# The first batch and the second batch's attention of a fused attention and mixing kernel, traced by a list schedule

## The chip, the cores and the metric

The kernel runs on one core of one Trainium2 chip. The metric is the device time of one execution in microseconds (us). The engines are named as the profile names them: PE (matmuls), PEld (its weight loads), DVE, ACT, POOL (GpSimd) and SP, whose queue issues every DMA of this kernel.

## The reference

There are 8 batches of 576 tokens with 8 heads of 64, so 512 channels. Three stages follow each other:

```python
k_p, v_p = k, v averaged over 8 neighbouring tokens        # 72 keys per head
attn = softmax(q @ k_p.T / 8)
x = (attn @ v_p), heads side by side                        # 576 x 512 per batch
theta = x @ w_theta
y = w_tok_r @ (x * cos(theta)) + w_tok_i @ (x * sin(theta))
u = x + y
x = u + relu(u @ w_ch)
u = x + w_tok2.T @ relu(w_tok1.T @ x)                       # over the tokens
out = u + relu(u @ w_ch1) @ w_ch2
```

The weights of the mixing stages come as 64-bit floats. [...]

## The kernel before

Everything is traced by one Python function with the Tile framework, which derives the waits between engines and also chooses each engine's order: an instruction traced later can be placed ahead of one traced earlier, where Tile's own model finds the engine free. Every engine then works through its own list in order.

**Weights.** A weight is loaded in pieces of 128 rows by 256 or 288 columns: 8 of `w_theta` (`th`), 18 of `w_tok` (`tk`, 9 row blocks in two column halves). Each piece goes through one conversion, in `cq_ahead` and `cq_step`: ACT takes the absolute value of the high word (L223); a guard keeps it at 2^-15 or above, for these 26 pieces by a Relu with bias on ACT (L225) and an addition on POOL (L226); DVE shifts and masks (L256), puts the sign in (L262) and the low word's three bits (L268). A `tk` piece is then split into a high part (ACT, L294) and a low part `m - hi` (L296); two thirds of the low parts go to POOL, one third to DVE (`lo_engine`). The later weights (`w_ch` and on) take their guard on DVE, by a maximum (L253).

**One batch.** `emit_sc` multiplies queries by a block diagonal of summed keys (`bdk`), takes the row maximum (DVE, L539), subtracts it (DVE, L540) and exponentiates (ACT, L545), four times for two heads each; `emit_norm` sums (DVE, L552) and scales (POOL, L557); `emit_pt` transposes on PE, `emit_av` multiplies by the values into `R`. `emit_theta` gives theta for 5 groups (half 0: groups 2, 0, 1; half 1: groups 0, 1); `emit_z` transposes `R` and multiplies it by cosine and sine (DVE, L758), and splits the product into high (ACT, L772) and low parts (L773, POOL or DVE). The mix is 8 accumulations of 27 matmuls (`mix_part`) over `Z` and the split `w_tok`, added to `R` on DVE (L811) and stored. Batch 0 uses plain 32-bit matmuls for attention and theta; from batch 1 on high and low parts are multiplied apart.

**Order.** `prologue` traces batch 0 up to `Z` of half 0, with the conversion of pieces spread between by counts (`P["pq"]`). PE fills some waits with matmuls on a constant tile (`keep_busy`, L169). Then comes a loop over the batches: the 72 steps of `mix_steps(b)` are the main line, and everything else (theta and `Z` of half 1 of batch b; attention, theta and `Z` of half 0 of batch b+1; loads and sums of keys and values of batch b+2) is a side list with due times from `P`, put between the steps by `interleave`. For batch 0 the due times are those of `f_`. After the last batch the channel mixing of w_ch, the second token mix and the two large channel products follow.

**Buffers.** There is one home for each tag. Raw pieces stay in `Z0`, `kr`, `stg0`, `stg1`, `R1`, `w0` to `w3` and `Z1` until they are converted; batch 1's keys come into `Xl` when batch 0's values are pooled, its values into `R1`. There are 8 PSUM banks: 4 `x`, 2 `t`, 2 `m`.

Of the kernel before, what the change touches and what calls it, by code (L numbers as in the profile page):

```python
# [9 lines left out]
F32 = mybir.dt.float32  # L10
# [34 lines left out]
    "pl": (2.0, 2.0, 0, 0.0),  # L45
    "l_cq": (1.26, 1.0),
    "l_u": (11.67, 22.91, 4.84),
    "l_th1": (3.39, 3.6),
# [4 lines left out]
    "a_th": (0,),  # L53
    "a_tr": 4,
    "md": (1.7, 2.0),
    "pq": (2.0, 2.0, 2.0, 2.0, 3.6, 2.0, 2.0, 2.0, 2.0, 2.0, 20.0),
    "mo": 1,
}
F64_FLOOR = 2.0 ** -15
TH = ((0, 256), (256, 320))  # L60
HL3 = ((0, 0), (0, 1), (1, 0))


@with_exitstack
def tile_attn_moe(
# [11 lines left out]
    w_ch1: bass.AP,  # L77
    w_ch2: bass.AP,
    consts: bass.AP,
    k1: bass.AP,  # L80
    v01: bass.AP,
    pool: bass.AP,
    out: bass.AP,
# [111 lines left out]
    def cq_use(stages, cvts):  # L195
        cq_bufs[:] = list(stages)
        cvt_bufs[:] = list(cvts)
# [1229 lines left out]
            second_chunk(c)  # L1427


    def prologue():  # L1430
        z0 = st("Z0", [128, 7, CV, 2], U32, "early0")
        z1 = st("Z1", [128, 6, CV, 2], U32, "early")
        r1 = st("R1", [128, 4, CV, 2], U32, "early2")
        kr = st("kr", [128, 2, CV, 2], U32, "early4")
        zt = st("zt1", [128, 3, CV], F32, "early3")
        cv = st("vr", [128, 3, CV], F32, "early5")
        ws = [st(W_TAGS[i], [128, CV, 2], U32, f"early_w{i}") for i in range(4)]
        cq_use([(z0[:, i],) for i in range(7)] + [(kr[:, i],) for i in range(2)] + ["stg0", "stg1"]
               + [(r1[:, i],) for i in range(4)] + [(w,) for w in ws] + [z1[:, i] for i in range(6)],
               ["cvt0"] + [zt[:, i] for i in range(3)] + [cv[:, i] for i in range(3)])  # L1440
        pq = [int(x + 0.5) for x in P["pq"]]
        pl = [int(x + 0.5) for x in P["pl"]]
        add_wth()
        add_wtk()
        kt = {}
        for p in range(4):
            if p % 2 == 0:
                kt[p // 2] = st(f"pt{p // 2}", [128, 2, T], F32, f"k{p // 2}")
                q_t[0, p // 2] = st(f"q{p // 2}", [128, 2, TD], F32)
            nc.sync.dma_start(out=kt[p // 2][:, p % 2], in_=kT[0, p])  # L1450
            nc.sync.dma_start(out=q_t[0, p // 2][:, p % 2], in_=qT[0, p])
            cq_load(pl[p])
        load_pool()
        load_n(0, vn_t, "Xl", v01[0])
        cq_load()
        for p in range(4):
            ks = st("sums", [128, 72], F32)
            nc.vector.tensor_reduce(
                out=ks, in_=kt[p // 2][:, p % 2].rearrange("p (k o) -> p k o", o=8), axis=AX.X, op=ALU.add
            )  # L1460
            for e in range(2):
                pr = slice(64 * e, 64 * e + 64)
                nc.vector.tensor_copy(out=bdk[pr, p, 72 * e:72 * e + 72], in_=ks[pr])  # L1463
            emit_sc(0, p)
            if p > 0:
                emit_norm(0, p - 1)
        pool_v(0)
        emit_norm(0, 3)
        pool_vl(0)
        cq_step(pq[0])  # L1470
        emit_pt(0, 4)
        emit_pt(0, 0)
        for j in range(4):
            if j < 3:
                emit_pt(0, j + 1)
            flush()
            for th in range(2):
                emit_av(0, j, th)
            cq_step(pq[1 + j])
        flush()  # L1480
        cq_step(pq[5])
        emit_theta(0, 0, 2)
        emit_theta(0, 0, 0)
        cq_step(pq[6])
        flush()
        emit_z(0, 0, 2, nc.gpsimd)
        emit_theta(0, 0, 1)
        cq_step(pq[7])
        flush()
        emit_z(0, 0, 0, nc.gpsimd)  # L1490
        cq_step(pq[8])
        flush()
        emit_z(0, 0, 1, nc.vector)
        flush()
        cq_step(pq[9])
        if B > 1:
            open_vlo()
            for g in range(2):
                load_q(1, g)
            load_n(1, kn_t, "Xl", k1)  # L1500
            load_n(1, vn_t, "R1", v01[1])
        cq_step(pq[10])

    def side_first():
        ft = P["f_prep"]
        return [
            (ft[0], lambda: pool_k(1, 0)),
            (ft[1], lambda: pool_k(1, 1)),
            (ft[2], lambda: pool_v(1)),
            (ft[3], lambda: pool_vl(1)),  # L1510
        ] + [(P["f_ws"][0] + i * P["f_ws"][1], lambda i=i: split_wth(i)) for i in range(4)]

    def side_next(b):
        n = b + 1
# [24 lines left out]
        ]  # L1539

    if True:
        prologue()
        for b in range(B):
            last = b == B - 1
            side = []
            f = "l_" if last else "f_" if b == 0 else ""
            for g, a, z, lo in zip((0, 1), P[f + "th1"], P[f + "z1"], (nc.gpsimd,) * 2):
                side.append((a, lambda g=g: emit_theta(b, 1, g)))
                side.append((z, lambda g=g, lo=lo: emit_z(b, 1, g, lo)))
            if not last:  # L1550
                side += side_next(b)
            if b + 2 < B:
                side += side_load(b + 2)
            if b == 0 and not last:
                side += side_first()
# [68 lines left out]
def _layout(inputs):  # L1624
# [25 lines left out]
    for r in range(128):  # L1650
# [9 lines left out]
        "consts": consts, "k1": nat[0][1], "v01": nat[1], "pool": pool,  # L1660
    }


# [20 lines left out]
```

## Time and profile before

| | |
|---|---|
| median of 3 runs | 1298.02 us (1297.08 to 1298.23) |
| the profiled execution's own time | 1297.42 us |
| its span, first to last instruction | 1295.6 us |
| busy: PE, DVE, ACT, POOL | 1254.6, 956.9, 661.0, 321.9 us |
| the chain that ended last | PE 76%, DVE 9%, DMA 2% |

A busy engine is one with an instruction running. The timeline merges neighbouring instructions of one kind into one row (xN), with its start, its length, and the idle time ahead of it in brackets with what ended it. Each 32-bit matmul leaves two records. Rows of neighbouring instructions overlap a little, since an instruction's end is later than the next one's start.

### The profile page before, as it was taken

The page shows a single profiled execution, that of the slowest core. Times are in us where ns is not written, and L with a number is a line of the kernel's source. Part 1 is how long each engine was busy: PE and PEld are TensorE (multiplying, and loading weights), DVE is VectorE, ACT ScalarE, POOL GpSimd, SP SyncE. Part 2 cuts the span into 40 slices and gives each one's busy share as a digit, 9 for nine tenths or more (in the row PEclk, how much of TensorE's full clock was granted, in tenths as well). Part 3 has the DMA queues.
Part 4 walks back from the last instruction along what each step waited for, and adds up shares of the span by engine and source line. Part 5 has one row for each costly group of instructions (what it writes and reads, how often), then busy time and mean ns, then how long its engine had stood idle before and what let it go on. Part 6 is the DMA issues. An engine that isn't in the chain of part 4 may idle for free.

```text
span 1295.6 us, 22271 instructions
## 1 busy us (share of the span) xinstructions
PE 1254.6 (97%) x8130; PEld 1209.8 (93%) x8132; DVE 956.9 (74%) x1730; ACT 661.0 (51%) x1256; POOL 321.9 (25%) x339
## 2 busy tenths in 40 slices
PE   5799999999999999999999999999999999999998
PEld 4489999999999988899999998999999999999998
DVE  7888577585857796686775689996545598987893
ACT  4776565666666573333331356655544444444442
POOL 4643425232332532111110012320000032123122
PEclk9899999999999999999999999999999999999999
DMA  9424233231321023556683388885438966547621
GB/s 338 158 71 138 74 100 103 75 94 62 115 73 52 36 93 109 181 199 233 246 297 116 128 273 281 281 280 178 146 123 279 367 215 224 172 142 218 196 91 62
DMA packets 120382, 214.50 MB, mean 166 GB/s; under 512 B 11536, under 2 KB 66320, under 8 KB 120272
## 3 DMA queue, kind: packets, MB, share of 16 engines
q1 hardware_dynamic: 120272, 213.08, 49.2%
q8 instruction: 64, 1.05, 0.3%
q14 instruction: 46, 0.38, 0.1%
HBM read 134.39 MB, written 78.64 MB: 164 GB/s over the span
## 4 chain that ended last, share of the span: by engine, by line
PE 76%; DVE 9%; DMA 2%; issue 2%; ACT 2%; POOL 0%; SPq 0%; ACTq 0%; DVEq 0%; POOLq 0%
PE m L159 28%; PE x L159 25%; PE t L159 19%; PE x L173 3%; DMA ws<-w_ch 1%; DMA scr_x<-u 1%; DVE wm L1024 1%; DVE raw_n L1155 1%; DVE wm L1028 1%; DVE wsum L1039 0%; DVE p L1313 0%; DVE g L1323 0%; ACT wo L1052 0%; DVE ope_R L1152 0%; ACT wm L1018 0%
## 5 line engine op out<-in xcount | busy, mean ns | idle before, releaser
L159 PE MATMUL m<-wtk,Z 128*128 128x256 f32 (+1 forms) x1536 | 253.6, 301 | 4.6 <-ACT Z L772 3.0
L159 PEld LDWEIGHTS m<-wtk,Z 128*128 128x128 f32 x1536 | 220.2, 190 | 6.1 <-ACT Z L772 3.2
L773 POOL TENSOR_TENSOR Z<-tmp,Z 128x1024 fp32r<-128x1024 f32 x31 | 74.9, 2415 | 112.1 <-ACT Z L772 112.1
L159 PE MATMUL x<-ope_Z,wa 128*128 128x384 f32 x492 | 95.4, 337 | 0.0
L1404 POOL TENSOR_TENSOR o<-o,u 128x384 f32<-128x384 f32 x12 | 16.3, 1379 | 285.5 <-DVE u L1392 218.0
L159 PEld LDWEIGHTS x<-ope_Z,wa 128*128 128x128 f32 x492 | 86.8, 188 | 0.1
L1038 POOL TENSOR_TENSOR wsum<-wm 128x128 f32<-128x128 f32 (+1 forms) x18 | 15.1, 840 | 272.4 <-DVE wm L1028 264.8
L758 DVE TENSOR_TENSOR tmp<-x,tmp 128x1024 f32<-128x1024 f32 x32 | 39.1, 1221 | 33.4 <-ACT tmp L734 17.8
L159 PE MATMUL t<-wth,Xh 128*128 128x256 f32 x448 | 62.9, 282 | 0.0
L159 PE MATMUL x<-bdk,q 128*128 128x144 f32 x320 | 47.8, 303 | 11.5 <-DVE bdk L1463 7.0
L159 PEld LDWEIGHTS t<-wth,Xh 128*128 128x128 f32 x448 | 57.9, 188 | 0.9 <-DVE tmp L709 0.2
L159 PEld LDWEIGHTS x<-bdk,q 128*128 128x128 f32 x320 | 44.5, 203 | 13.1 <-issue 10.9
L159 PE MATMUL m<-wtk,zt 128*128 128x256 f32 (+1 forms) x192 | 56.8, 296 | 0.0
L557 POOL TENSOR_TENSOR e<-e,sm 128x720 f32<-128x720 f32 x32 | 44.7, 1398 | 20.8 <-DVE sm L556 18.7
L159 PE MATMUL t<-ope_Z,wa 128*128 128x384 f32 x234 | 48.2, 336 | 1.5 <-ACT p L1312 1.5
L159 PE MATMUL m<-ope_Z,wa 128*128 128x384 f32 x234 | 48.2, 336 | 0.0
L740 DVE SCALAR_TENSOR_TENSOR tmp<-tmp,t 128x512 f32<-128x512 f32 x33 | 22.5, 683 | 31.3 <-ACT tmp L727 31.3
L545 ACT ACTIVATE e<-e 128x720 f32<-128x720 f32 x32 | 25.6, 804 | 38.0 <-DVE e L540 37.9
L159 PE MATMUL x<-ope_R,wa 128*128 128x384 f32 x228 | 44.1, 338 | 0.4 <-DVE p L1317 0.3
L811 DVE TENSOR_TENSOR R<-m,R 128x256 f32<-128x256 f32 (+1 forms) x64 | 28.8, 450 | 20.2 <-PE m L159 20.2
L772 ACT CAST Z<-tmp 128x1024 fp32r<-128x1024 f32 x32 | 33.4, 1043 | 20.0 <-DVE tmp L758 20.0
L159 PE MATMUL m<-ope_Xl,wa 128*128 128x384 f32 x204 | 42.9, 338 | 0.6 <-ACT ope_Xl L1151 0.6
(406 smaller groups left out, 3546.3 us busy)
## 6 DMA issues: line engine op xcount, KB each, us to landing
wa<-scr_w SPq DMA_DIRECT2D x42, 512.0 KB, 5.6
scr_g<-g SPq DMA_DIRECT2D x108, 192.0 KB, 3.0
scr_w<-wo SPq DMA_DIRECT2D x42, 256.0 KB, 3.0
scr_u<-R SPq DMA_DIRECT2D x32, 288.0 KB, 2.1
u<-scr_u SPq DMA_DIRECT2D x32, 288.0 KB, 4.0
scr_w<-wo SPq DMA_DIRECT2D x18, 512.0 KB, 3.4
scr_x<-u SPq DMA_DIRECT2D x32, 288.0 KB, 2.4
raw_n<-scr_x SPq DMA_DIRECT2D x24, 384.0 KB, 4.3
```

The lines of the kernel that those rows point to most:

```text
L159: nc.tensor.matmul(out=o, lhsT=l, rhs=r, start=start, stop=stop, skip_group_check=skip)
L173: nc.tensor.transpose(o, i, ident)
L545: nc.scalar.activation(out=ep, in_=ep, func=ACTF.Exp, scale=1.0 / 64.0)
L557: nc.gpsimd.tensor_tensor(out=ep, in0=ep, in1=sm.unsqueeze(3).to_broadcast([128, 5, 2, 72]), op=ALU.mult)
L740: nc.vector.scalar_tensor_tensor(out=t, in0=t, scalar=MAGIC, in1=pt, op0=ALU.subtract, op1=ALU.subtract)
L758: nc.vector.tensor_tensor(out=tmp, in0=px.unsqueeze(1).to_broadcast([128, 2, 512]), in1=tmp, op=ALU.mult)
L772: nc.scalar.copy(out=zh, in_=zv)
L773: later(1.0 if lo is nc.vector else 0.0, lambda: lo.tensor_sub(out=zl, in0=zv, in1=zh.bitcast(F32)), tg, zg)
L811: nc.vector.tensor_add(out=R[:, j, ts], in0=o, in1=R[:, j, ts])
L1024: nc.vector.scalar_tensor_tensor(out=xu, in0=t[:, :, :, 1], scalar=0xC0000000, in1=xu, op0=ALU.bitwise_and, op1=ALU.bitwise_or,)
L1038: nc.gpsimd.tensor_tensor(out=s[:, 2], in0=a11, in1=a21, op=ALU.subtract)
L1404: nc.gpsimd.tensor_tensor(out=u22[d].t, in0=u22[d].t, in1=u2[d].t, op=ALU.add)
```

## The change

`prologue` and batch 0's turn of the batch loop, with its side list, are replaced by `first_batches`. It describes the whole work of batch 0 (attention, the 26 pieces, theta and `Z` of both halves, the mix, its stores), the split of `w_theta`, and of batch 1 loads, attention, theta and `Z` of half 0, with the loads of batch 2's queries and its key sums, as operations with dependencies, a duration in ns, an engine (sometimes a choice of two), the buffers and the banks they take. `Plan.run` goes through time in that model: of all operations that could start within 20 ns of the earliest, it traces the one with the longest chain behind it. POOL operations and DVE operations marked `True` aren't started together (`lock`). Afterwards each instruction of PE, DVE, ACT and POOL gets a dependency without a semaphore on the one traced before it on its engine; SP's don't. Values of batch 2 are loaded and summed behind the last of them (`issue_after`), and the batch loop starts at batch 1.

What the operations are differs from before in this: all 26 guards are one DVE maximum (`GUARD`), so L225 and L226 have none left; all 18 low parts of `tk` are on POOL (`LOWS` is empty); of batch 0's half 0 all three low parts of `Z` are on DVE (`ZL`), the scaling of head pairs 2 and 3 of batch 0 is on DVE (`EDVE`); small copies out of PSUM are on DVE or ACT as the plan finds it. `keep_busy` fills the waits of PE that the plan foresees up to the first mix matmul, and the time ahead of the first matmul. Keys of batch 1 are loaded in four column blocks. The host passes both batches' natural keys (`k01`).

```diff
+GUARD = range(26)
+LOWS = ()
+WS = (0, 1)
+ZL = (1, 1, 1)
+EDVE = (2, 3)
+NEAR = 20.0
...
-    def prologue():
...
+        LAT = {"PE": 170.0, "DVE": 110.0, "ACT": 120.0, "POOL": 110.0, "SP": 0.0}
...
+                    for w in o["ways"]:
+                        if w[0] == "SP":
+                            if sp:
+                                continue
+                            sp = True
+                        s = max(ready, free[w[0]], lock + (90.0 if w[0] == "POOL" else 0.0) if w[2] is True else 0.0)
+                        d = w[1]
+                        if w[2] in ("exp", "sin") and w[2] != table:
+                            d += 1290.0
+                        best.append((s, s + d, o, w))
+                s0 = min(b[0] for b in best)
+                near = [b for b in best if b[0] <= s0 + NEAR]
+                top = max(b[2]["rank"] for b in near)
...
+                if e == "PE":
+                    idle(s, s - free["PE"])
...
+                if e == "SP" and w[2]:
+                    self.dma = max(self.dma, s + 3000.0) + w[2] * 1000.0 / 370.0
+                    o["end"] = self.dma
...
+    def first_batches():
...
+        def idle(s, ns):
+            if started[0] is False:
+                started[0] = True
+                keep_busy(dump, int((s - WARM) / 440.0))
+            elif started[0]:
+                keep_busy(dump, int(max(0.0, ns - 60.0) / 217.0))
...
+            o = add(("ACT", ac(n), False, absf), [at], hs, take=mids)
+            if i in GUARD:
+                o = add(("DVE", n * 0.521 + 65, True, most), [o], hs)
...
+            o = add(("DVE", n * 0.521 + 65, True, shl), [o], hs)
+            o = add(("DVE", dv(n), True, sign), [o], hs)
+            o = add(("DVE", dv(n), True, low3), [o], hs)
...
+            x = add(("ACT", ac(n), False, hi), [o], hs + [w], give=[hold])
+            ways = [("POOL", po(n), True, low(nc.gpsimd))]
+            if i in LOWS:
+                ways = [("DVE", dv(n), True, low(nc.vector))]
...
+        for p in range(4):
+            scores(0, p)
+        for i in range(8):
+            add_piece(i)
+        values(0)
+        transposed(0, 4)
         for j in range(4):
...
+        for i in range(8, 26):
+            add_piece(i)
+        for g in TG:
+            theta(0, 0, g)
+        for g in range(2):
+            theta(0, 1, g)
+
+        fetch_q(1)
+        kn[1] = home("Xl", [128, 5, 512], F32, "nat_k1")
+        kt_at[1] = fetch_tail(kn[1], k01[1])
+        for p in range(4):
+            fetch_k_pair(1, p)
+            fetch_q_pair(1, p)
+        fetch_v(1, "R1")
...
+        pl.run(idle)
...
+        for i in nc.cur_bb.bb.instructions[first:]:
+            k = str(i.engine)
+            if "SP" in k:
+                continue
+            if k in seen:
+                tc.add_manual_dep(i, seen[k], mybir.DependencyInfo(
+                    mybir.DependencyClass.NoSync, mybir.DependencyReason.DATA), reason="the plan's order")
...
     if True:
-        prologue()
-        for b in range(B):
+        behind = first_batches()
+        with ExitStack() as s:
+            for i in behind:
+                s.enter_context(tc.issue_after(i))
+            if B > 2:
+                load_v(2, 0)
+                load_vl(2)
+                prep_v(2, 0)
+                load_v(2, 1)
+                prep_v(2, 1)
+                prep_vl(2)
+            flush()
+        for b in range(1, B):
```

## Rows read from the trace of the kernel before

**Rows 1.** The page's 40 slices of 32.4 us: busy tenths of PE.

```profile
PE   5799999999999999999999999999999999999998
```

**Rows 2.** Busy time of each engine by stretch; a stretch, its length, engines with counts.

```profile
core 0: us, PE busy (x) PEld busy (x) DVE busy (x) ACT busy (x) POOL busy (x), PEclk, DMA share, GB/s
0.00:78.20 78.20, 57.21 (x244) 40.56 (x247) 65.87 (x150) 50.08 (x111) 44.13 (x64) 0.95 0.63 214
78.20:142.01 63.81, 62.30 (x435) 57.40 (x434) 47.93 (x89) 39.00 (x78) 24.35 (x24) 0.99 0.34 108
142.01:205.00 62.99, 62.95 (x491) 62.01 (x490) 40.41 (x79) 38.38 (x75) 19.84 (x20) 1.00 0.27 87
445.00:505.00 60.00, 54.51 (x401) 52.77 (x400) 53.99 (x130) 34.43 (x74) 23.64 (x28) 0.97 0.31 102
```

**Rows 3.** Timeline of PE, 0 to 80 us: start, length, instruction, idle ahead.

```profile
5.50 2.74 PE L159 MATMUL x<-bdk,q 128*128 128x144 f32 x10 [5.50 <-DVE bdk L1463]
...
22.72 1.39 PE L159 MATMUL x<-bdk,q 128*128 128x144 f32 x10
...
40.32 0.59 PE L169 MATMUL x<-busy 128*128 128x512 bf16 x2
40.75 0.38 PE L173 MATMUL x<-con,e 128*128 128x128 f32 x2
...
55.88 7.61 PE L159 MATMUL t<-wt,R 128*128 128x512 f32 x18 [5.77 <-DVE R L523]
...
64.44 3.72 PE L159 MATMUL t<-wt,R 128*128 128x256 f32 x16 [0.51 <-DVE tmp L740]
...
78.21 0.99 PE L159 MATMUL m<-wtk,Z 128*128 128x256 f32 x2
```

**Rows 4.** Timeline of PE from 139 us on: the first matmul behind batch 0's mix.

```profile
142.01 1.11 PE L159 MATMUL t<-wth,Xh 128*128 128x256 f32 x8
```

**Rows 5.** Groups of PE, 0 to 142.01 us: busy us, mean ns, idle before.

```profile
L169 PE MATMUL x<-busy 128*128 128x512 bf16 x38 | 11.0, 379 | 1.2 <-ACT pt L588 1.2
...
L159 PE MATMUL x<-nat_Xl,pool 128*128 128x512 f32 (+1 forms) x10 | 5.8, 712 | 0.2 <-PE x L159 0.2
```

**Rows 6.** Groups of DVE, 0 to 142.01 us.

```profile
L256 DVE TENSOR_SCALAR early<-early 128x288 uint32<-128x288 uint32 (+1 forms) x22 | 9.0, 422 | 0.0
...
L552 DVE TENSOR_REDUCE ss<-e 128x10 f32<-128x720 f32 x8 | 7.1, 897 | 1.0 <-ACT e L545 1.0
...
L296 DVE TENSOR_TENSOR wtk<-early,wtk 128x288 fp32r<-128x288 f32 x6 | 4.9, 818 | 3.8 <-ACT wtk L294 3.8
...
L430 DVE TENSOR_REDUCE vls<-vlr 96x64 f32<-96x512 f32 x6 | 4.0, 675 | 0.5 <-POOL vlsh L434 0.5
L398 DVE TENSOR_REDUCE sums<-kr 128x144 f32<-128x1152 f32 x3 | 4.0, 1346 | 0.0
...
L408 DVE TENSOR_REDUCE sums<-vr 128x128 f32<-128x1024 f32 x2 | 2.4, 1214 | 0.0
...
L773 DVE TENSOR_TENSOR Z<-tmp,Z 128x1024 fp32r<-128x1024 f32 x1 | 1.2, 1210 | 0.0
```

**Rows 7.** Groups of ACT, 0 to 142.01 us.

```profile
L225 ACT ACTIVATE early<-early,floor 128x288 f32<-128x288 f32 (+1 forms) x22 | 11.2, 523 | 0.2
```

**Rows 8.** Groups of POOL, 0 to 142.01 us.

```profile
L226 POOL TENSOR_SCALAR early<-early 128x288 f32<-128x288 f32 (+1 forms) x22 | 13.6, 622 | 17.6 <-ACT early L225 17.3
...
L296 POOL TENSOR_TENSOR wtk<-early,wtk 128x288 fp32r<-128x288 f32 x10 | 8.8, 896 | 0.8 <-ACT wtk L294 0.8
...
L226 POOL TENSOR_SCALAR cvt<-cvt 128x256 f32<-128x256 f32 (+1 forms) x4 | 3.2, 799 | 5.5 <-ACT cvt L225 5.5
```

**Rows 9.** Timeline of DVE: one guard of a later weight.

```profile
77.53 2.33 DVE L253 TENSOR_SCALAR cvt<-cvt 128x256 f32<-128x256 f32 x1
```

**Rows 10.** Timeline of POOL at the same time.

```profile
77.31 2.41 POOL L773 TENSOR_TENSOR Z<-tmp,Z 128x1024 fp32r<-128x1024 f32 x1
```

**Rows 11.** Timeline of SP's queue: the load of batch 1's values.

```profile
51.66 0.89 SPq L457 DMA_DIRECT2D nat_R<-v  x2
```

More of the change, by code (lines that the diff above doesn't have):

```diff
@@ L60 @@
 TH = ((0, 256), (256, 320))
+TG = (2, 0, 1)
+GUARD = range(26)
+NK = 4
+WARM = 800.0
+LOWS = ()
[3 more added lines that the diff above has]
+NEAR = 20.0
 HL3 = ((0, 0), (0, 1), (1, 0))
@@ L1504, in side_first, with __init__, add, home @@
[L1504 to L1511, printed above, removed]
+    class Plan:
+        LAT = {"PE": 170.0, "DVE": 110.0, "ACT": 120.0, "POOL": 110.0, "SP": 0.0}
+        def __init__(self):
+            self.ops = []
+            self.users = {}
+            self.dma = 3400.0
+        def add(self, ways, deps=(), homes=(), take=None, give=()):
+            if isinstance(ways, tuple):
+                ways = [ways]
+            o = dict(ways=ways, deps=list(deps), take=take, give=give)
+            for h in homes:
+                o["deps"] += h.prior
+                h.users.append(o)
+            self.ops.append(o)
+            return o
+        def home(self, tag, shape, dt, name=None):
+            return Home(self, tag, shape, dt, name)
+        def run(self, idle):
+            table = None
+            for o in self.ops:
+                o["rank"] = 0.0
+            for o in reversed(self.ops):
+                e, ns = o["ways"][0][0:2]
+                o["rank"] += (ns if e != "SP" else 2000.0) + self.LAT[e]
+                for d in o["deps"]:
+                    d["rank"] = max(d["rank"], o["rank"])
+            free = {e: 0.0 for e in self.LAT}
+            lock = 0.0
+            todo = list(self.ops)
+            while todo:
+                best = []
+                sp = False
+                for o in todo:
+                    if any("end" not in d for d in o["deps"]):
+                        continue
+                    ready = max([0.0] + [d["end"] for d in o["deps"]])
+                    if o["take"] is not None:
+                        if not o["take"].free:
+                            continue
+                        ready = max(ready, o["take"].free[0][0])
+                    for w in o["ways"]:
+                        if w[0] == "SP":
+                            if sp:
+                                continue
+                            sp = True
[7 more added lines that the diff above has]
+                top = max(b[2]["rank"] for b in near)
+                o = [b[2] for b in near if b[2]["rank"] == top][0]
+                s, end, o, w = min((b for b in best if b[2] is o), key=lambda b: b[1])
+                todo.remove(o)
+                e = w[0]
+                if e == "PE":
+                    idle(s, s - free["PE"])
+                free[e] = end
+                if w[2] is True:
+                    lock = end
+                elif w[2] is not False and e == "ACT":
+                    table = w[2]
+                o["end"] = end + self.LAT[e]
+                if e == "SP" and w[2]:
+                    self.dma = max(self.dma, s + 3000.0) + w[2] * 1000.0 / 370.0
+                    o["end"] = self.dma
+                if o["take"] is not None:
+                    o["take"].last = o["take"].free.pop(0)[1]
+                w[3]()
+                for g in o["give"]:
+                    g.done(o["end"])
@@ new lines, in tile_attn_moe, with __init__, __call__ @@
+    class Home:
+        def __init__(self, plan, tag, shape, dt, name):
+            self.prior = plan.users.get(tag, [])
+            self.users = plan.users[tag] = []
+            self.args = (tag, shape, dt, name)
+            self.t = None
+        def __call__(self):
+            if self.t is None:
+                self.t = st(*self.args)
+            return self.t
+    class Slots:
+        def __init__(self, names):
+            self.free = [(0.0, n) for n in names]
+            self.last = None
@@ L1553, in tile_attn_moe @@
                 side += side_load(b + 2)
-            if b == 0 and not last:
-                side += side_first()
             if last:
@@ L1659, in _layout @@
         "w_ch1": w["moe2_w_ch1"], "w_ch2": w["moe2_w_ch2"],
-        "consts": consts, "k1": nat[0][1], "v01": nat[1], "pool": pool,
+        "consts": consts, "k01": nat[0], "v01": nat[1], "pool": pool,
     }
```

688 lines of the change are left out of this document (618 added, 70 removed).

## The prediction

> **What bounds the kernel now.** I began with the slices: PE is at nine tenths almost everywhere, and the large hole is in the first two [rows 1]. The windows then place it. From 142.01 us on PE is busy 62.95 of 62.99 us [rows 2], so the kernel is a PE line with a ragged start, and what the start loses moves the end one for one. The boundary at 142.01 is the first matmul of batch 1's turn, behind the last of batch 0's mix [rows 4]; 78.20 is where that mix begins [rows 3]. A later hole, 445 to 505 us, where PE is busy 54.51 of 60 and DVE 53.99 [rows 2], belongs to the last batch; the change does not touch it and it only shifts.
>
> Next I asked how much of the first 142.0 us is work of PE that has to be done. Busy are 57.21 + 62.30 = 119.5 us [rows 2], so 22.5 are idle. Of the busy time some is no work:
> - The filler matmuls: 38 of them [rows 5], and two take 40.75 - 40.32 = 0.43 us [rows 3], so 38 x 0.215 = 8.2 us.
> - The slow clock: the scores of the first head pair take 2.74 us, those of the last 1.39 [rows 3]. Three pairs ran slow, 3 x 1.35 = 4.0 us. The theta block at 55.88 us comes behind 5.77 us of idling and takes 7.61; at the pace of the one at 64.44 (16 records of 256 columns in 3.72 us, 0.23 each) its 8 records of 512 and 10 of 256 would be 26 x 0.23 = 6.0. That is 1.6 more.
>
> So 119.5 - 8.2 - 5.6 = 105.7 us are work and **36.3 us are not**. The reason is in the groups and the timeline of DVE's neighbours: PE waits for DVE (at 5.50 for `bdk`, at 55.88 for `R`, at 64.44 for `tmp` [rows 3]), and DVE is busy 65.87 of the first 78.20 us, against 50.08 of ACT and 44.13 of POOL [rows 2]. In the second stretch DVE is at 47.93 of 63.81 while PE is full. The two engines take turns as the bound: about 114 us of DVE work and 106 us of PE work in 142. Better overlap of these two is what the plan could give.
>
> **The change part by part.** All edits act on that start, so I price DVE and PE up to the new place of 142.01, which I call T.
>
> *DVE, removed.* Six low parts go to POOL, 6 x 0.818 = 4.9 us [rows 6]. Work for later batches that was placed inside the first 142 us isn't in the plan, or follows it by `issue_after`: six value sums of 0.675 (4.0), one of the three key sums of 1.346 (1.3, the plan keeps batch 2's two), two value sums of 1.214 (2.4) [rows 6], and the w_ch guard of 2.33 [rows 9]. Together 10.0. This comes later, where DVE has slack (40.41 busy of 62.99 us [rows 2]) under a full PE; if that cover were gone it would cost at most its own 10.0 back.
>
> *DVE, added.* 26 guards. No guard of these pieces ran on DVE before. From below: nothing, where DVE would have waited. From above: 2.33 us each, the one later guard I see [rows 9], 60.6 in all. The nearest row is the shift of the same pieces, also one input and one output of the same size, at 0.422 us [rows 6]; I take it: 26 x 0.422 = 11.0. Two low parts of Z more on DVE: 1.210 for the one with 1024 columns [rows 6] and half of it for the one with 512, 1.8. Two scalings of 720 columns, at the 0.897 of the sum over the same 720 [rows 6]: 1.8. The choice of engine for small copies I cost at nothing, since it goes either way and ACT has room.
>
> DVE's sum: 113.8 - 4.9 - 10.0 + 11.0 + 1.8 + 1.8 = 113.5 us. So the title's edits hardly change DVE's load; what changes is its idling, 28.2 us of the 142 before.
>
> *ACT and POOL.* ACT loses the Relus, 11.2 us for 22 of 26 [rows 7]. POOL loses 26 additions, 13.6 + 3.2 = 16.8, and gains 6 x 0.896 = 5.4 [rows 8], and hands the two Z parts and two scalings to DVE. Neither is the bound (89 and 68 of 142 us [rows 2]), so both are worth nothing by themselves. They take two engine crossings from each piece's chain, so DVE finds its next piece ready.
>
> *PE.* The work stays 105.7 us. The warm-up before the first matmul and the fillers in foreseen waits cost nothing while DVE is the bound, and spare the 5.6 us of slow clock; the cover is PE's own idling, and where the plan foresees a wait that isn't there, one filler costs 0.215.
>
> *SP.* The same bytes, with two DMAs more for keys and values and a tiny one for the pool matrix ahead of the first keys. I cost the tiny one at its own issue, at most half of the 0.89 for a pair [rows 11], 0.4 us, on the path to the first scores. Batch 1's loads need homes that are freed by conversions, as before.
>
> **Two floors for T.** DVE: it starts near 4.5 us (PE's first matmul at 5.50 waits for it) and needs 113.5, so T is 118 at the least. PE: in the first 30 us it has only scores (4 x 1.39 = 5.6 [rows 3]) and the pooling of values (5.8 [rows 5]), 11 us, since everything else waits for the softmax; the other 94.7 follow, so T is 125 if it is never idle behind 30 us, and some 121 if the plan brings the softmax forward by 4 us, which DVE's sum allows because no conversion need stand in its way. Before, the loss behind 30 us was 142.0 - 30 - 94.7 = 17.3 us. I assume that the plan leaves 5 of it above the floor of 121, as 26 pieces, PSUM banks and two `tmp` tiles still couple the engines. **T = 126, a gain of 16 us**: 1297.42 of the profiled execution becomes 1281.4; the median of the runs is 0.6 above that execution, so 1282.0.
>
> **A rule weighed.** A guard of 256 columns that began at 77.53 us took 2.33 us and ended at 79.86; beside it POOL ran a subtraction from 77.31 to 79.72 [rows 9, 10]. So a DVE instruction can stand until POOL's ends. The Trainium skill, "SBUF — State Buffer", section "SBUF: two separate sides", says that DVE and GpSimd share one port pair under an exclusive lock held for a whole instruction, and that DVE takes it in its 2-port modes or with two SBUF inputs against a GpSimd instruction that reads SBUF. By that rule all four DVE steps of a piece, not only the guard, stop for each low part. It speaks against putting all low parts on POOL; the trace agrees in this one pair of rows. By the rule T is rival 1's below. My sum leaves collisions at the rate already in the 0.422 and gives 126.
>
> **The rivals.**
> 1. *Each low part on POOL stops DVE for its whole length.* 18 x 0.896 = 16.1 us [rows 8] on top of 113.5, so DVE's floor is 134 and T about 135: a gain of 7, 1291. For it: rows 9 and 10. Against it: the 26 additions, which collided too, leave POOL, and the plan keeps the marked operations apart, so that POOL can work while DVE reads PSUM. Chance 0.12. The Trainium skill's rule above gives this time wherever the plan's durations don't hold on the chip.
> 2. *The change doesn't do what it says for the order.* The added dependencies order only the plan's own instructions. Tile can still put later batches' sums between them, as it did (six of 0.675, for instance). Then DVE gets its 10.0 back and order is no better coordinated: T 136 to 142, a gain of 0 to 6, 1292 to 1298. Chance 0.12, a third of it within the noise.
> 3. *Slower: PE stands behind a transfer of batch 1.* PE works its list in order. The plan puts batch 1's keys and values wherever its model of the DMAs (370 GB/s, 3 us) lets them be, possibly ahead of theta or of the mix. The values were issued at 51.66 us [rows 11], because `R1` had to be emptied of four pieces; if PE reached them at 30 and they come near 55, it stands 25 us with all of theta queued behind it. T would be 151, 9 us slower: 1307. It decides once such waits exceed the 16 us of my gain. For it: SP's queue is in order too, and one late conversion delays all loads behind. Against it: the plan's chain lengths put theta and conversions first, and all pieces but a few arrive well before they are needed. Chance 0.11.
> 4. *Better: PE full from 25 us on*, T 118 or less, DVE at its floor: 1273 or less. Chance 0.07.
>
> **How the numbers follow.** The forecast, 1274 to 1290, has 0.58. Faster by over 0.2% (2.6 us, about what a measurement here can tell from no change): 0.58 + 0.07 + 0.12 + two thirds of 0.12, so 0.85. Within 0.2%: 0.05. Slower: 0.10 (a hundredth of rival 3 lies within the noise). The range reaches to 1271 below (T = 115, under both floors by little) and to 1298 above, which takes in rivals 1 and 2 and leaves out rival 3 and the far end of rival 4.
>
> **What would show it.** Right: the first mix matmul some 10 us earlier or more, batch 1's scores and key pooling ahead of it, the first matmul of batch 1's turn near 126, no PE idling of 5 us behind 30, first scores at 1.4 rather than 2.7 us, L225 and L226's successors on DVE near 0.4 us, and behind T the pace of before. Wrong: guards and shifts near 1 us (rival 1), later batches' sums among the plan's (rival 2), a PE wait on a DMA (rival 3). The forecast fails if DVE still idles over 20 us before T, or if PE's line behind T is longer than before.

## The result, and the profile after

The changed kernel takes **1275.4 us** (median of 4 runs, 1274.72 to 1276.8) against 1298.01 of the kernel before in the same job: ratio 0.983, 95% interval 0.981 to 0.985. The forecast was 1282.0, between 1271 and 1298. The profiled execution took 1276.8 us; its span, from the first to the last instruction, is 1275.0.

The page's slices of PE (40 of 31.9 us), which answer to [rows 1]; the dip at the fifteenth slice is the later hole of batch 7, now 20 us earlier:

```profile
PE   8999999999999989999999999999999999999998
```

Busy time by stretch in the changed kernel: a stretch, its length, then PE, PEld, DVE, ACT and POOL with their counts, the granted TensorE clock, the DMA share and GB/s. 52.39 us is the first mix matmul (before 78.21), 121.78 the first matmul of batch 1's turn, which the prediction called T (before 142.01 [rows 4]).

```profile
0.00:52.39 52.39, 47.20 (x216) 31.20 (x216) 43.67 (x115) 33.20 (x83) 13.79 (x20) 1.00 0.90 295
52.39:121.78 69.39, 67.43 (x463) 62.50 (x464) 55.63 (x119) 48.33 (x108) 33.64 (x25) 0.98 0.24 77
...
0.00:121.78 121.78, 114.63 (x678) 93.69 (x679) 99.31 (x233) 81.52 (x190) 47.42 (x44) 0.99 0.52 171
...
22.97:121.78 98.81, 95.07 (x594) 83.39 (x594) 83.57 (x193) 71.98 (x167) 43.02 (x35) 0.98 0.43 137
...
121.78:185.00 63.22, 61.15 (x460) 59.59 (x459) 48.28 (x92) 38.84 (x79) 22.18 (x25) 0.97 0.42 131
425.00:485.00 60.00, 54.43 (x392) 52.66 (x391) 53.89 (x133) 31.39 (x70) 26.06 (x28) 0.94 0.29 91
```

**Where the gain is.** T came 142.01 - 121.78 = 20.2 us earlier, and the span is 1295.6 - 1275.0 = 20.6 us shorter; behind T the line is as long as before (1295.6 - 142.0 = 1153.6, now 1153.2). Up to T, PE idled 142.0 - 119.5 = 22.5 us before [rows 2] and 121.8 - 114.6 = 7.2 now, which is 15.3 us; the other 4.9 are busy time (119.5 to 114.6) with as many records (679 before, where those at 78.20 count twice, and 678 now), of which 38 and 40 are fillers. So the same matmuls were done faster: the slow scores are gone, and the clock fell less. All the idling that went stood ahead of the first mix matmul: 78.2 - 57.2 = 21.0 us before, 52.4 - 47.2 = 5.2 now.

The timeline of PE in the changed kernel shows both, and what stands behind T:

```profile
5.72 1.48 PE L167 MATMUL x<-bdk,q 128*128 128x144 f32 x10 [0.59 <-ACT bdk L1768]
...
22.97 1.23 PE L181 MATMUL x<-con,e 128*128 128x128 f32 x9
...
36.03 7.07 PE L167 MATMUL x<-wt,R 128*128 128x256 f32 x32
...
52.39 0.62 PE L167 MATMUL m<-wtk,Z 128*128 128x256 f32 x3 [1.08 <-ACT Z L2193]
...
57.53 1.50 PE L167 MATMUL t<-pool,nat_k 128*128 128x16 f32 x12
...
61.31 0.90 PE L167 MATMUL x<-bdk,q 128*128 128x144 f32 x6
...
121.78 1.10 PE L167 MATMUL t<-wth,Xh 128*128 128x256 f32 x8
...
133.62 1.42 PE L167 MATMUL x<-bdk,q 128*128 128x144 f32 x6 [2.06 <-DVE tmp L766]
```

The first scores take 1.48 us where they took 2.74 [rows 3]; the transposes of the softmax begin at 22.97, and batch 1's key pooling (57.53) and scores (61.31) now stand behind the first mix matmul; theta runs 32 matmuls in one row (7.07 us, 0.22 each) with no wait ahead of it, where 5.77 us of idling stood before. The longest wait between 36 us and T is the 1.08 at the first mix. Behind T a new wait of 2.06 us has come, for DVE's `tmp`. In the kernel before, the transposes began 5.8 us later than now:

```profile
28.76 0.38 PE L173 MATMUL x<-con,e 128*128 128x128 f32 x2
```

The groups of DVE from 0 to 121.78 us (line, operation, tiles, shapes, count, then busy us, mean ns, idle before), which answer to [rows 6]: the guard (L1697), the shift (L1708), and two of the five steps of a w_ch piece (L276, L261).

```profile
L1697 DVE TENSOR_SCALAR early<-early 128x288 f32<-128x288 f32 x16 | 5.1, 339 | 1.1 <-ACT early L1694 1.1
L1708 DVE TENSOR_SCALAR early<-early 128x288 uint32<-128x288 uint32 x16 | 4.7, 327 | 0.0
...
L1697 DVE TENSOR_SCALAR early<-early 128x256 f32<-128x256 f32 x6 | 1.5, 283 | 0.0
...
L276 DVE SCALAR_TENSOR_TENSOR cvt<-stg,cvt 128x256 uint32<-128x256 uint32 x1 | 1.4, 1389 | 0.0
...
L261 DVE TENSOR_SCALAR cvt<-cvt 128x256 f32<-128x256 f32 x1 | 1.2, 1212 | 0.0
```

The group of POOL that answers to the second of [rows 8], the low part:

```profile
L1741 POOL TENSOR_TENSOR wtk<-early,wtk 128x288 fp32r<-128x288 f32 x16 | 18.5, 1173 | 33.1 <-ACT wtk L1738 31.4 <-DVE tmp L2180 1.7
```

### The profile page after: what moved, and what is told of

The parts are those of the page before. It is cut to its first block, busy times and chain, and to the rows that moved or that the text cites. A ratio compares the mean times of both kernels' runs of the same rounds, so it can differ in the third digit from the quotient of the medians.

```text
span 1275.0 us, 22259 instructions
## 1 busy us (share of the span) xinstructions
PE 1248.5 (98%) x8132; PEld 1205.9 (95%) x8132; DVE 953.2 (75%) x1739; ACT 656.4 (51%) x1264; POOL 302.7 (24%) x301
## 4 chain that ended last, share of the span: by engine, by line
PE 76%; DVE 11%; DMA 7%; ACT 2%; issue 2%; SPq 1%; POOL 0%; DVEq 0%; ACTq 0%; POOLq 0%
PE m L167 28%; PE x L167 26%; PE t L167 19%; PE x L181 3%; DMA ws<-w_ch 1%; DMA early<-w_tok 1%; DMA scr_x<-u 1%; DMA early<-w_theta 1%; DMA scr_w<-wo 1%; DMA k<-kT 1%; DMA q<-qT 0%; DMA vr<-vm 0%; DMA scr_g<-g 0%; DVE early L1713 0%; DMA stg<-w_ch 0%
## 5 line engine op out<-in xcount | busy, mean ns | idle before, releaser
L167 PE MATMUL m<-wtk,Z 128*128 128x256 f32 (+1 forms) x1536 | 259.6, 304 | 5.7 <-ACT Z L780 3.0
L167 PE MATMUL x<-ope_Z,wa 128*128 128x384 f32 x492 | 94.8, 336 | 0.0
L781 POOL TENSOR_TENSOR Z<-tmp,Z 128x1024 fp32r<-128x1024 f32 x26 | 62.9, 2419 | 86.7 <-ACT Z L780 86.7
L766 DVE TENSOR_TENSOR tmp<-x,tmp 128x1024 f32<-128x1024 f32 x26 | 31.7, 1220 | 28.9 <-ACT tmp L742 15.5
L167 PE MATMUL x<-bdk,q 128*128 128x144 f32 x298 | 42.9, 293 | 2.7 <-DVE tmp L766 2.1
L167 PEld LDWEIGHTS x<-bdk,q 128*128 128x128 f32 x298 | 39.4, 194 | 4.2 <-DVE tmp L766 2.3
L167 PEld LDWEIGHTS x<-ope_R,wa 128*128 128x128 f32 x228 | 41.6, 194 | 1.5 <-DVE p L1325 1.5
L167 PEld LDWEIGHTS t<-ope_Z,wa 128*128 128x128 f32 x234 | 41.3, 188 | 1.6 <-ACT p L1320 1.6
L167 PE MATMUL t<-ope_Xl,wa 128*128 128x384 f32 x204 | 42.5, 336 | 0.0
L167 PE MATMUL x<-ope_Xh,wa 128*128 128x384 f32 x192 | 39.4, 336 | 2.5 <-DVE p L1325 1.3
L167 PEld LDWEIGHTS m<-ope_Z,wa 128*128 128x128 f32 x234 | 41.5, 188 | 0.0
```

The source lines that it names most:

```text
L167: nc.tensor.matmul(out=o, lhsT=l, rhs=r, start=start, stop=stop, skip_group_check=skip)
L766: nc.vector.tensor_tensor(out=tmp, in0=px.unsqueeze(1).to_broadcast([128, 2, 512]), in1=tmp, op=ALU.mult)
L781: later(1.0 if lo is nc.vector else 0.0, lambda: lo.tensor_sub(out=zl, in0=zv, in1=zh.bitcast(F32)), tg, zg)
```

## The experiments

**Theory A**: the gain comes from the plan, that is from the overlap of batch 0's pieces with batch 1's attention, in an order that is enforced. **Theory B**: it comes from the edits that can be made without a plan: guards on DVE, low parts on POOL. One measure runs through all runs below: T, and next to it what the fallen clock cost up to T. For that I took windows of 2 us and summed PE's busy time times (1 - granted clock); the sum is an estimate. "T less" is their difference. The records read 1.00 while the first scores ran slow (e6, below), so the column leaves that out in the kernel before, e1, e2 and e6. One profile stands behind each row, and the ratios are to the kernel before in the same job. T of the changed kernel came out within 0.3 us in its two profiles; the stretch behind T lies between 1150.5 (e3) and 1156.0 us (e6), so small differences are read from T and not from the time.

| kernel | median us | ratio, 95% | first mix | T | clock | T less |
|---|---|---|---|---|---|---|
| before | 1298.01 | | 78.2 | 142.0 | 3.5 | 138.5 |
| after | 1275.4 | 0.983, 0.981 to 0.985 | 52.4 | 121.8 | 1.7 | 120.1 |
| after, again (r_after_again) | 1274.6 | 0.983, 0.981 to 0.985 | 52.1 | 121.5 | 1.7 | 119.8 |
| e1, before with guards on DVE | 1301.5 | 1.003, 1.001 to 1.004 | 74.7 | 144.9 | 6.5 | 138.5 |
| e2, and low parts on POOL | 1302.3 | 1.004, 1.002 to 1.005 | 74.6 | 145.1 | 6.6 | 138.5 |
| e3, order not enforced | 1281.6 | 0.986, 0.984 to 0.989 | 56.5 | 128.7 | 4.8 | 123.9 |
| e4, guards as before | 1276.4 | 0.983, 0.981 to 0.985 | 52.3 | 123.1 | 0 | 123.1 |
| e5, low parts on DVE | 1283.0 | 0.988, 0.986 to 0.990 | 51.4 | 131.5 | 9.0 | 122.5 |
| e6, one filler | 1278.1 | 0.985, 0.983 to 0.987 | 55.0 | 124.6 | 1.7 | 122.9 |
| e7, no lock in the plan | 1281.1 | 0.987, 0.986 to 0.989 | 53.0 | 127.0 | 6.6 | 120.3 |
| e8, value sums later | 1274.2 | 0.981, 0.980 to 0.982 | 51.9 | 120.8 | 1.7 | 119.1 |
| e9, and nothing between | 1274.9 | 0.982, 0.981 to 0.984 | 52.0 | 119.8 | 0 | 119.8 |
| e10, four weight pieces later | 1276.5 | 0.983, 0.982 to 0.985 | 48.9 | 121.4 | 3.4 | 118.0 |
| e12, fillers ahead of the keys | 1283.1 | 0.988, 0.986 to 0.990 | 50.3 | 130.3 | 9.2 | 121.1 |

### The two edits alone, in the kernel before

e1 has the 26 guards on DVE and the order as before:

```diff
-    cq_mode = [0]
+    cq_mode = [1]
```

> The kernel before with one part of the change alone: the 26 guards are one DVE maximum, so the 26 Relus (L225) and POOL additions (L226) go. Theory A (the gain is overlap: the plan's order lets PE and DVE work at the same time) expects little, 1294 to 1300, because DVE's load grows by 26 x 0.32 = 8 us and the order stays. Theory B (the gain is in the edits: shorter chains per piece) expects most of the 22.6 us, 1285 or less.

e2 is the same with all low parts on POOL:

```diff
-    lo_m = [3]
+    lo_m = [1000]
```

> The kernel before with both edits of the title: guards on DVE and all 18 low parts of w_tok on POOL, order by due times as before. Theory A: 1293 to 1300. Theory B: 1282 or less. If the low parts on POOL stop DVE for their length, it is slower than the run with the guards alone by up to 6 x 0.9 = 5 us.

Both came out 0.3 to 0.4% **slower**. e2 lies 0.8 us above e1, and their intervals overlap. The mix began 3.5 us earlier, and batch 1's turn 3 us later. The windows of e1 up to the mix and up to T show where that went, against [rows 2]:

```profile
0.00:74.71 74.71, 55.15 (x212) 38.12 (x214) 61.75 (x161) 36.43 (x78) 29.08 (x35) 0.93 0.63 215
74.71:144.91 70.20, 68.45 (x466) 62.53 (x466) 55.84 (x104) 42.71 (x86) 28.48 (x27) 0.98 0.33 107
```

PE idled 21.3 us, 1.2 less than before, but was busy 4.1 us longer (123.6 against 119.5) with one record less: the clock fell at four places instead of two. Without the clock's share all three kernels have T at 138.5. So theory B falls, and the edits alone are worth nothing in this order. The guard that I had no row for took 633 ns on average here (a group of DVE in e1, 0 to 142 us). Of all 22 guards on these tiles the median is 304 ns and the longest 2467, so the mean comes from a few long ones:

```profile
L253 DVE TENSOR_SCALAR early<-early 128x288 f32<-128x288 f32 x16 | 9.8, 633 | 0.0
```

### The plan without one of its parts

**The enforced order (e3).** The plan traces in its order, and Tile may move instructions again:

```diff
-            if k in seen:
-                tc.add_manual_dep(i, seen[k], mybir.DependencyInfo(
-                    mybir.DependencyClass.NoSync, mybir.DependencyReason.DATA), reason="the plan's order")
```

> The changed kernel without the dependencies that keep each engine to the plan's order; the instructions and the order in which they are traced are the same. Theory A1 (the gain needs the enforced order): Tile's own model moves instructions and 8 us or more are lost, 1284 or more. Rival A2 (the traced order is enough): within 3 us of the changed kernel's 1275.4.

It lies between what the two versions of theory A expected: 6 us slower than the changed kernel and 16 faster than the one before. PE's waits now stand at the first mix and at batch 1's transposes (timeline of PE in e3):

```profile
56.53 0.83 PE L167 MATMUL m<-wtk,Z 128*128 128x256 f32 x3 [3.76 <-ACT Z L2193]
...
92.66 0.55 PE L181 MATMUL t<-con,e 128*128 128x128 f32 x3 [1.24 <-POOL e L1865]
```

Of T's 6.9 us, 3.8 are order and 3.1 the clock. Describing the work anew is worth more than enforcing its order: 16 of the 22.6 us stay. No run splits these 16 further, since none keeps the plan's loads, fillers and choice of engines and gives up its order as it is traced.

**The guards (e4)** on ACT and POOL as before, within the plan:

```diff
-GUARD = range(26)
+GUARD = ()
```

> The changed kernel with the guards as before, a Relu on ACT and an addition on POOL, planned anew by the same scheduler. Theory A expects 1276 to 1281: ACT takes 13 us and POOL 17 us more, DVE 8 us less, and PE, which is the bound from 28 us on, only feels later pieces. Theory B expects 1286 or more.

The time can't be told from the changed kernel's, as theory A expected. T is 1.3 us later in this profile; the clock never fell in it, so its order is some 3 us worse and its clock 1.7 better. That split is one profile's and no more than an estimate.

**The low parts (e5)** on DVE:

```diff
-LOWS = ()
+LOWS = range(26)
```

> The changed kernel with all 18 low parts of w_tok on DVE instead of POOL, planned anew. If PE is the bound behind 28 us and DVE has slack (99.3 us busy of the 121.8 before batch 1's turn), DVE takes 18 x 0.37 to 18 x 0.8 = 7 to 14 us more and the time stays within 4 us of the changed kernel's 1275.4, 1275 to 1279. If DVE is the bound, 1282 to 1290.

7.6 us slower than the changed kernel, which lies in the range for DVE as the bound. DVE is busy 106.5 us up to T, 7.2 more, but T is 9.7 later: 2.4 without the clock's share, 7.3 by the clock. It fell twice, from 58 to 67 us (3.4 us) and from 72 to 87 (5.6), the second time in the longest wait (timeline of PE in e5):

```profile
75.61 5.61 PE L167 MATMUL x<-pool,nat_k 128*128 128x16 f32 x24 [5.47 <-DVE tmp L2125]
81.15 1.33 PE L167 MATMUL t<-bdk,q 128*128 128x144 f32 x4
```

PE waits 5.47 us for DVE, and what follows runs at half the clock: 24 key poolings take 5.61 us, where 12 take 1.50 to 1.60 at the full clock (e10, below).

**The fillers (e6)**, all but one at the start left out:

```diff
             if started[0] is False:
                 started[0] = True
-                keep_busy(dump, int((s - WARM) / 440.0))
-            elif started[0]:
-                keep_busy(dump, int(max(0.0, ns - 60.0) / 217.0))
+                keep_busy(dump, 1)
```

> The changed kernel without the filler matmuls (one is left ahead of everything). If the clock falls without them and that matters: scores at 2.7 us instead of 1.4 (4 pairs, some 5 us, partly on the path) and values and transposes slower, 1279 to 1284. If the first 28 us are set by DVE and the arrival of keys and queries alone: within 2 us of 1275.4.

2.7 us slower by the medians, between the two expectations. The two intervals overlap, but T is 2.8 us later. The scores take 2.74 us again (timeline of PE in e6), although the records give a clock of 1.00 there:

```profile
5.63 2.74 PE L167 MATMUL x<-bdk,q 128*128 128x144 f32 x10 [3.70 <-ACT bdk L1766]
10.76 2.77 PE L167 MATMUL t<-bdk,q 128*128 128x144 f32 x10 [2.39 <-ACT bdk L1766]
```

**The lock term (e7)**: the plan no longer keeps POOL's and the marked DVE operations apart.

```diff
-                        s = max(ready, free[w[0]], lock + (90.0 if w[0] == "POOL" else 0.0) if w[2] is True else 0.0)
+                        s = max(ready, free[w[0]])
```

> The changed kernel whose plan lets DVE and POOL operations start together (no lock). If collisions cost what the rule of the shared port says (each stops the other for its length) and the plan avoids them by that term: low parts on POOL and guards get longer and 3 us or more are lost, 1278 or more. If the term decides nothing because PE is the bound: within 2 us of 1275.4.

5.7 us slower, and DVE does stand: the sign steps of a `tk` piece take 728 ns (449 in the changed kernel) and POOL's low parts 1082 (1173). The group of DVE in e7, 0 to 127 us:

```profile
L1713 DVE SCALAR_TENSOR_TENSOR early<-early,early 128x288 uint32<-128x288 uint32 x12 | 8.3, 728 | 0.0
```

and that of POOL:

```profile
L1741 POOL TENSOR_TENSOR wtk<-early,wtk 128x288 fp32r<-128x288 f32 x16 | 16.9, 1082 | 10.5 <-ACT wtk L1738 10.5
```

But PE's idle time up to T hardly grew (7.5 us, from 7.2). It was busy 4.8 us longer with the same matmuls, because the clock fell three times instead of once. Two of the falls come right behind waits that are longer than in the changed kernel (1.08 and 0.45 us there; timeline of PE in e7):

```profile
53.01 0.69 PE L167 MATMUL m<-wtk,Z 128*128 128x256 f32 x3 [2.18 <-ACT Z L2193]
...
72.69 1.84 PE L167 MATMUL x<-pool,nat_k 128*128 128x16 f32 x12 [2.63 <-DVE tmp L2125]
```

So the lock term is worth 5 us here, and they came by the clock.

### What is left in T

**Batch 2's value sums (e8)** are traced behind the plan and stand, traced early, ahead of batch 1's `tmp`. The DVE timeline of the changed kernel behind T shows a sum that waits 3.00 us for its DMA, with PE's 2.06 us wait behind it:

```profile
130.12 1.22 DVE L416 TENSOR_REDUCE sums<-vr 128x128 f32<-128x1024 f32 x1 [3.00 <-DMA vr<-vm]
131.70 0.61 DVE L423 TENSOR_TENSOR vbl<-sums,vbh 64x128 fp32r<-64x128 f32 x2 [0.36 <-ACT vbh L430]
132.34 1.22 DVE L766 TENSOR_TENSOR tmp<-x,tmp 128x1024 f32<-128x1024 f32 x1
```

```diff
-                prep_v(2, 1)
                 prep_vl(2)
...
+            if b == 1 and B > 2:
+                side.append((10.0, lambda: prep_v(2, 1)))
```

> The changed kernel with the second value sum of batch 2 moved from right behind the plan into batch 1's side list at 10 us. In the changed kernel DVE stood 3.0 us on that load at 130 us and PE 2.06 us behind it. If that wait is what PE pays: 1273.0 to 1274.0, some 2 us less. If another wait ends last there, or the value sum collides with the softmax of batch 2 later: 1275 to 1277.

> The changed kernel once more, beside the next two on the same chip, so that differences of 1 to 3 us can be told: ratio to the kernel before 0.981 to 0.985, T (the first matmul of batch 1's turn) within 1 us of 121.8 us.

1274.2, the lowest median of all, beside 1274.6 for the changed kernel in a further run, whose ratio and T (121.5) came as expected: the intervals overlap, so a gain isn't shown, though PE's wait did shrink to 1.22 + 0.42 us.

**Nothing between (e9)** is e8 with every later instruction ordered behind the plan, which takes the hoisted w_ch steps out of it:

```diff
+        for i in behind:
+            ctx.enter_context(tc.issue_after(i))
```

> The kernel with the later value sum, and in addition every instruction behind the plan is held behind the plan's last one on its engine, so that the first conversion steps of w_ch, 5 us of DVE in the changed kernel, can't stand between the plan's. If they delay DVE where PE waits for it: T 1 to 3 us earlier, 1271 to 1273. If DVE had the room, as it has 18 us of idling before T: no difference from the kernel with the later value sum.

T moved by 1.0 us and the time did not: the span behind T grew by 2.3 (1273.1 - 119.84 = 1153.3, after e8's 1271.8 - 120.84 = 1151.0), which is within the spread of that stretch. The wait on DVE came back there (timeline of PE in e9):

```profile
131.51 1.00 PE L167 MATMUL x<-bdk,q 128*128 128x144 f32 x6 [1.89 <-DVE tmp L766]
```

**An earlier softmax (e10)**: e8, with the four weight pieces that are loaded between the first head pairs' keys and queries loaded behind them.

```diff
-    "pl": (2, 2, 0, 0),
+    "pl": (0, 0, 0, 0),
```

> The kernel with the later value sum, and in addition the four weight pieces (1.05 MB) that are loaded between the head pairs' keys and queries come behind them. If PE is the bound from the first transposes on, and these wait for a softmax that waits for keys: queries of the last pair land some 2.8 us earlier, transposes and T 1.5 to 3 us earlier, 1270 to 1272. If DVE's softmax work is what sets the transposes, or the theta pieces now come late: no gain or up to 1 us slower.

The transposes began at 20.39 instead of 22.62 us and the mix 3.1 us earlier (48.92 against 52.06 in the run of the changed kernel beside it), yet T came at 121.36, and 1276.5 lies above both expectations. All engines in windows of 2 us in e10 (the granted clock is the third number from the end):

```profile
58.00:60.00 2.00, 2.00 (x16) 1.95 (x15) 1.89 (x6) 2.00 (x5) 0.00 (x0) 0.86 0.00 0
60.00:62.00 2.00, 2.00 (x10) 1.98 (x10) 2.00 (x8) 1.90 (x8) 0.00 (x0) 0.50 0.00 0
...
64.00:66.00 2.00, 2.00 (x11) 2.00 (x11) 2.00 (x5) 1.10 (x3) 2.00 (x2) 0.50 0.00 0
```

The timeline of PE in e10 ahead of these windows, in them and behind:

```profile
55.12 1.50 PE L167 MATMUL x<-pool,nat_k 128*128 128x16 f32 x12
56.55 1.60 PE L167 MATMUL t<-pool,nat_k 128*128 128x16 f32 x12
...
58.54 1.91 PE L167 MATMUL x<-pool,nat_k 128*128 128x16 f32 x12
...
61.19 1.64 PE L167 MATMUL x<-bdk,q 128*128 128x144 f32 x6
...
70.06 0.90 PE L167 MATMUL x<-bdk,q 128*128 128x144 f32 x6
```

PE is busy all the time, and its clock falls behind the pooling of the keys: six score records take 1.64 us, and 0.90 after it has risen. Without the clock's share T would be 118.0, 1.1 less than e8's. The rest of the 3.1 seems to have gone into waits at 85.62 (1.18 us, for DVE's `R`) and 91.55 (0.48); no run shows it.

**Fillers ahead of the key pooling (e12)** were to hold the clock in e10 (the plan also counts each pooling 434 ns longer):

```diff
                 o = box["o"] = bank_of(hold)
+                keep_busy(o, 2)
```

> The kernel of e10_qk_first with two filler matmuls ahead of each of batch 1's four key poolings (8 x 0.215 = 1.7 us of PE more). If it was the fallen clock behind the key pooling that gave back the 3.1 us by which e10's mix began earlier: the granted clock stays at 1.00 from 58 to 66 us, the mix still begins near 49, and batch 1's turn begins 2 to 3 us less the 1.7 before e10's 121.4, so at 119.5 to 121; time 1274 to 1276. If something else takes the gain back (waits that end last further on): the clock is restored or not, and batch 1's turn begins at 121.4 or, with the fillers' 1.7 on top, at 123; time 1276 to 1278.

A miss, outside both expectations: 1283.1. The clock fell again, some 2 us later, and stayed low for longer. The first window of 2 us with the fallen clock in e12, and the last at 0.50 of that stretch (a second, from 88 to 95 us, comes behind the longest wait):

```profile
60.00:62.00 2.00, 2.00 (x11) 1.52 (x10) 2.00 (x8) 1.96 (x6) 0.00 (x0) 0.62 0.00 0
...
72.00:74.00 2.00, 2.00 (x10) 2.00 (x10) 1.75 (x5) 0.99 (x3) 0.48 (x1) 0.50 0.04 12
```

Of PE's timeline in e12, fillers and key pooling before and behind the fall, and the longest wait:

```profile
58.35 0.60 PE L177 MATMUL t<-busy 128*128 128x512 bf16 x2
58.79 1.50 PE L167 MATMUL t<-pool,nat_k 128*128 128x16 f32 x12
...
60.82 1.08 PE L177 MATMUL x<-busy 128*128 128x512 bf16 x2
61.69 2.68 PE L167 MATMUL x<-pool,nat_k 128*128 128x16 f32 x12
...
89.98 2.50 PE L167 MATMUL m<-wtk,Z 128*128 128x320 f32 x8 [3.78 <-DVE R L2274]
```

Two fillers take 0.60 us ahead of the fall and 1.08 behind it. The clock cost 9.2 us in place of 3.4, the fillers 1.7, and a wait of 3.78 us for DVE's `R` stands at 89.98. That the clock is what gave back e10's gain isn't shown by this run, since it failed to keep it; e10's own windows show that it fell, and a way to keep it was not found.

## Why the prediction held, point by point

**What bounds the kernel: right.** The start was ragged by two engines that took turns, and what it lost moved the end one for one (20.2 us at T, 20.6 in the span, nothing behind T). The later hole only shifted: PE 54.43 of 60 us now, 54.51 before [rows 2].

**The floor of PE: right, and the terms can be checked.** Against 30 less 4 us to the softmax, 94.7 of work behind it and 5 of loss, the trace has 22.97, 95.07 and 98.81 - 95.07 = 3.74, which sum to 121.78. **The mis-sized step** is thus "some 121 if the plan brings the softmax forward by 4 us": it began 7.0 before the 30, which is 3.0 of the 4.2 us by which I was off. Of these 3.0, some 1.2 are the 30 itself, since the transposes of the kernel before began at 28.76; the plan brought them forward by 5.8. The second is "I assume that the plan leaves 5 of it above the floor": 3.7. That 94.7 meets 95.07 is partly luck: the 95.07 hold five fillers (1.1 us) and 1.7 of slow clock, so the work was some 92.3. The prediction had overlooked the second fall of the clock in the kernel before, from 76 to 80 us, which is 1.7 of the difference. The median differs by 6.6 from the forecast: 4.2 at T, 0.4 behind it, and 2.0 in the distance from the profiled execution to the median, which I took over as +0.6 and which is -1.4 here (1276.8 and 1275.4).

**DVE's sum: too large by 14.2 us** (113.5 against 99.3), so DVE's floor of T was some 104 and not 118. Two terms account for most of it. The guards, "26 x 0.422 = 11.0", take 283 to 339 ns, and neighbouring ones follow each other at 0.22 us. The timeline of DVE in the changed kernel shows that a row's length is not what the engine spends:

```profile
60.03 0.30 DVE L1697 TENSOR_SCALAR early<-early 128x288 f32<-128x288 f32 x1
60.25 0.30 DVE L1697 TENSOR_SCALAR cvt<-cvt 128x288 f32<-128x288 f32 x1
...
60.69 0.81 DVE L1713 SCALAR_TENSOR_TENSOR early<-early_w,early 128x288 uint32<-128x288 uint32 x2
```

26 x 0.22 = 5.7, an estimate, so 5.3 less than I took. And the small copies, costed at nothing because "it goes either way", went one way: DVE had copies for some 9.0 us before T in the kernel before, and for 2.1 now. In time the guards are neutral: e4 shows no difference that can be measured.

**ACT and POOL "worth nothing by themselves": right** for the guards (e4), and e1 shows it in the old order too. The low parts on POOL were worth something: with all 18 on DVE (e5) T comes 9.7 us later for 7.2 of DVE's time, most of it by the clock. The 4.9 that I took off DVE's sum for six of them has no run of its own, since e5 moves all 18; the 18 took 447 ns each there, where the six took 818 [rows 6].

**Rival 1, POOL's low parts stop DVE: they did collide, but for less, and mostly POOL paid.** The low parts took 1173 ns each, against 896 before [rows 8] and 0.79 to 0.83 in the shortest rows of this trace: for the 16 of the group above some 5.5 us of POOL, an estimate (18.5 less 16 x 0.81), where rival 1 took 16.1 from DVE. The timeline of POOL in the changed kernel, beside DVE's conversion steps from 61.8 to 66.6 us, which kept their 0.30 and 0.45:

```profile
57.77 0.83 POOL L1741 TENSOR_TENSOR wtk<-early,wtk 128x288 fp32r<-128x288 f32 x1 [4.48 <-ACT wtk L1738]
63.44 6.17 POOL L1741 TENSOR_TENSOR wtk<-early,wtk 128x288 fp32r<-128x288 f32 x4 [4.84 <-ACT wtk L1738]
```

Four take 6.17 us there, 1.54 each. Steps outside the plan do stand: the five of the w_ch piece took 5.1 us between 87.02 and 93.78, beside POOL's scalings and a subtraction, with 1.21 for a guard whose size takes 0.28 in the plan. The Trainium skill, "SBUF — State Buffer", section "SBUF: two separate sides", says that of a GpSimd instruction and a DVE one (in a 2-port mode, or with two SBUF inputs where GpSimd reads SBUF) whichever starts first has the shared port pair for the whole instruction, and the other blocks. So the rule allows POOL as the one that stands, which the prediction left out; both directions are in these rows. e7 comes nearest to what rival 1 priced: DVE's sign steps rise to 728 ns, but its busy time up to T only by 3.7 us (103.0 against 99.3). Its T of 127 came by the clock.

**Rival 2, the order isn't as planned: in part.** Order that isn't enforced costs 6 us (e3), not the whole gain. The six value sums did leave, but one w_ch piece was still put between, 5.1 us of DVE; taking it out moved T by 1.0 and the time by nothing (e9).

**Rival 3, PE behind a transfer: not seen.** No wait of PE between the softmax and T ended on a DMA; the longest, 1.08 us, ended on ACT. **Rival 4**, T at 118, was not reached; e9 comes nearest with 119.8.

**Fillers "spare the 5.6 us": half.** They are worth some 2.7 (e6).

**The signs that were named: two came otherwise.** The first mix matmul came 26 us earlier, the first scores at 1.48, the guards at 0.28 to 0.34, and PE never idled 5 us between 30 us and T. But batch 1's key pooling and scores stand behind the first mix matmul, not ahead of it: the plan starts the mix early and fills it with batch 1's attention. And one sign of failure came true: DVE still idles 121.8 - 99.3 = 22.5 us before T, over the 20 that were named, and yet the time is in the range. I had expected DVE's load to stay and its idling (28.2) to go; the load fell by 14.5 us and the idling by 5.7. Where PE is the bound, DVE's idling is the wrong sign; PE's fell from 22.5 to 7.2.

**Is the lighter DVE the cause? At most in part.** What left DVE includes 7.7 us of sums for later batches. In the kernel before, only 2.0 of these stand ahead of the first mix matmul (at 67.57 and 71.55 us), the rest under a PE that is nearly full. e5 gives DVE 7.2 us back, and T, less the clock's share, comes 2.4 later; e9 takes 4.6 off (94.8 against 99.4 in e8), and T, less the clock's share, doesn't fall (119.8 against 119.1). The kernel before without that load was not run.

## What to carry to other kernels

Split a start into useful work, fillers and slow clock on the busiest engine, and forecast the end from the time at which its main work can begin, plus that work, plus the waits that stay. Price an instruction by its distance to the next of its kind, not by the length of its row. When variants differ by a few us, compare the granted clock window by window before arguing about order: in half of these runs it carried most of the difference in T.

## What the runs showed of the hardware

- **The granted clock fell to 0.50, the lower of its two levels (1.2 of 2.4 GHz), while the profile shows PE busy all the time**: behind runs of 16-column key poolings, from 60 to 66 us in e10 and from 62 to 74 in e12, with no wait of PE in the 8 us ahead. In the changed kernel it fell once up to T (0.80, 0.50 and 0.84 in the windows from 68 to 74), there behind waits of 0.24 and 0.45 us. In the profiles of e4 and e9 it didn't fall up to T with the same matmuls in another order, and two fillers ahead of each group did not hold it. What decides is open.
- Behind PE's longer waits it fell too: after 5.47 us in e5, 2.18 and 2.63 in e7, and after the 2.06 us behind T in the changed kernel, where the windows from 134 to 138 us have 0.52 and 0.63.
- The records of the clock don't show every slow stretch: they read 1.00 up to 24 us in e6 and in the kernel before, where ten score records take 2.74 us, against 1.39 later [rows 3].
- DVE's guard took 633 ns on average in e1 (median 304), 339 in the plan, and 2.33 us beside a POOL instruction of 2.41 [rows 9, 10]. Long ones in e1 begin just behind a POOL instruction and end about when it does: 1.37 us from 65.18 beside POOL's 64.91 to 66.39, 1.43 from 18.62 beside 18.51 to 19.90.
